# Retention and two feed-forward layers: GpSimd releases the products on zeros and decays one chunk of v, and a low half of x waits for chunk 3's output

## The chip, the core and the metric

The kernel runs on one core of a Trainium2 chip. The metric is the device time of one execution in microseconds (us), taken as the median of several runs. The core has TensorE (PE, with its weight loads PEld), VectorE (DVE), ScalarE (ACT), GpSimd (POOL) and SyncE (SP), which here only issues transfers. Each engine works through its own queue in order and waits on semaphores.

## What is computed

A retention layer (attention without a softmax, with a decay per head) is followed by two feed-forward layers, over 4608 tokens.

```python
rel = pos[:, None] - pos[None, :]
Dmat = np.where(rel >= 0, gamma[:, None, None] ** rel[None, :, :], 0.0)
ret = (scale * np.matmul(q, k.transpose(0, 1, 3, 2))) * Dmat[None]   # batch 8, heads 8, seq 576, dim 64
x = np.matmul(ret, v)  ->  [4608, 512]
h = x @ w_in;  x = (h - np.tanh(h)) @ w_out                           # layer 1, 512 -> 2048 -> 512
h = x @ w_in2; out = (h * (1 / (1 + np.exp(-1.702 * h)))) @ w_out2    # layer 2
```

## The kernel before

The sequence of each batch is cut into five chunks: four of 128 positions and one of 64. `chunks` lists them over all batches, so chunk 4 (counted from 0) is the last, short one of batch 0 and chunk 5 is the first of batch 1. For one chunk four functions run.

- `att_load` loads kT, qT, v and k into buffers of three each.
- `att_decay` multiplies v by a factor per position and head (`dg`). For the chunks 0, 1, 2, 5, 6 and 7 it is one multiplication on DVE (L295), for the others one ACT instruction per head (L300): eight for a chunk of 128, four for a chunk of 64.
- `att_scores` forms the products of k and q (`pj`, L316) and multiplies them by the mask on DVE (`pm`, L321). A "pin", a copy of one element into the bank ahead of the products (L311), ties the start of some chunks to another result: chunk 4 to the state S that chunk 3 leaves, chunk 5 to the first result `w` of the first feed-forward step.
- `att_values` adds the part that comes from the state S of the chunks before and the part within the chunk (`op`, L334), forms the next state (`up` on PE, L348, then two instructions on DVE, L352 and L353), and writes the output: the first 512 columns straight into `x_first` (`xf`, L362), later ones into `xe` (L367), which goes to memory (L371) and comes back as `yf` when its tile of 512 tokens is due (L388).

Four chunks (`LEAD`) run ahead of the feed-forward work. Between them PE is given products on a tile of zeros (`warm`), whose results nobody reads: `fill(src, n)` first writes a zero into one element of `warm`, as an ACT instruction that reads `src` (L719), and then issues n products of 512 columns (L722), which therefore can't run before `src` is there. After chunk 1 there are 5 of them, after chunk 3 there are 12, and `src` is the state S that the chunk just done leaves.

The feed-forward weights come as 64-bit floats in units. `unit_join` turns a unit into 32-bit floats (L176 and L180 on ACT, L178, L181 and L182 on DVE), `unit_split1` splits it into two 16-bit halves: the high half on ACT and the low half on DVE, both in `two` (L186 and L187). Names: `wih` and `wil` are the halves of the first matrix, `woh` and `wol` of the second. x is split in the same way into `xh` and `xl` by `whole(0)` (columns 0 to 383) and `whole(1)` (columns 384 to 511, which hold chunk 3's output).

The feed-forward steps then follow: `mm_in` forms `h` for a pair of blocks of 128 hidden units (24 products of 512 columns: high by high, high by low, low by high, L469), `act1` turns it into `gh` and `gl` on ACT and DVE (L482 to L487, L186, L187), and `mm_out` (L631) forms the output two steps later. The first pair needs the unit called (i, 0) here, that is the first one of the first matrix, the second pair the unit (i, 1). Beside the first tile's eight steps the remaining units are converted and the further chunks of the attention go on, chunk by chunk in one bank of PSUM (`late`). Tile 1 (tokens 512 to 1023) needs the output of the chunks 4 to 8.

The order of the instructions on each engine is not the program's order. It is set when the kernel is built, by a list scheduler that takes what its own estimate of the times calls ready, in the order of the program.

Of the kernel before, what the change touches and what calls it, by code (L numbers as in the profile page):

```python
# [17 lines left out]
AF = mybir.ActivationFunctionType  # L18
ALU = mybir.AluOpType
# [5 lines left out]
B, H, S, D = 8, 8, 576, 64  # L25
NT, DM, DFF = 4608, 512, 2048
P = 128
TT = 512
# [3 lines left out]
NPAIR = H // 2  # L32
# [23 lines left out]
LEAD = 4  # L56
# [39 lines left out]
def small_h(ctx: ExitStack, tc: tile.TileContext, w1i, w1o, w2i, w2o, qt, kt, k, v, dq_d,  # L96
            dv_d, mask_d, dg_d, out, flag):
    nc = tc.nc
    V, A, G, PE, SP = nc.vector, nc.scalar, nc.gpsimd, nc.tensor, nc.sync
# [25 lines left out]
    def pow2(mx, n, least, s, inv):  # L125

        p = scp.tile([P, n], F32, tag=f"p2_{n}", name="p2", bufs=3)
        V.tensor_scalar(out=p, in0=mx, scalar1=least, scalar2=None, op0=ALU.max)
        pi = p.bitcast(I32)
        V.tensor_scalar(out=pi, in0=pi, scalar1=EXPO, scalar2=None, op0=ALU.bitwise_and)  # L130
        V.tensor_scalar(out=s.bitcast(I32), in0=pi, scalar1=-1.0, scalar2=float((254 + 14) << 23),
                        op0=ALU.mult, op1=ALU.add)
        V.tensor_scalar(out=inv.bitcast(I32), in0=pi, scalar1=float(-(14 << 23)), scalar2=None, op0=ALU.add)

    def all_max(src, n, name):
        r = scp.tile([P, n], F32, tag=f"ar{n}", name=name, bufs=4)
        G.partition_all_reduce(r, src, P, RED.max)
        return r

    def most(dst, src, axis=AX.X):  # L140

        V.tensor_copy(out=dst, in_=newest[0])
        V.tensor_reduce(out=dst, in_=src, axis=axis, op=ALU.max, apply_absolute_value=True)
# [119 lines left out]
    att = {}  # L263
# [26 lines left out]
    def att_decay(b, n):  # L290
        s0, T = CHUNKS[n]
        a = att[b, n]
        if b * len(CHUNKS) + n in (0, 1, 2, 5, 6, 7):
            x, w = (0, H) if T == P else (H, NPAIR)
            V.tensor_tensor(out=a.v[:, :w], in0=a.v[:, :w], op=ALU.mult,  # L295
                            in1=dg[:, x : x + w].rearrange("p (a b) -> p a b", b=1).to_broadcast([P, w, D]))
            return
        for h in range(H if T == P else NPAIR):
            x = h if T == P else H + h
            A.activation(out=a.v[:, h], in_=a.v[:, h], func=AF.Copy, scale=dg[:, x : x + 1])  # L300
# [76 lines left out]
    def prep_steps(l, t):  # L377

        j = jobs[l, t] = Obj()

        def load():
            if (l, t) == (1, 0):
                j.src = x_first[0]
            else:
                j.src = yp.tile([P, KD, TT], F32, tag="yf", name=f"yf{l}_{t}")
                for x in range(2) if l == 1 else (slice(None),):
                    x = cut(x) if l == 1 else x
                    SP.dma_start(j.src[:, :, x], (x_d if l == 1 else y_d)[t][:, :, x])  # L388
            if l == 2:
                j.mx = scp.tile([P, 2], F32, tag="mx2", name="mxx", bufs=2)  # L390

        def cut(i):
            return (slice(0, 384), slice(384, TT))[i]

        def reduce(i):
            most(j.mx[:, i : i + 1] if l == 2 else xmost[:, 2 * t + i :][:, :1],
                 j.src[:, 2 * i : 2 * i + 2, :].rearrange("p a b -> p (a b)"))
            if i == 1 and l == 2:
                m1 = scp.tile([P, 1], F32, tag="mx1", name="m1", bufs=4)
                V.tensor_reduce(out=m1, in_=j.mx, axis=AX.X, op=ALU.max)  # L400
                j.r = all_max(m1, 1, "arx")

        def whole(i):
            if i == 0:
                j.xh = xp.tile([P, KD, TT], F16, tag="xh", name=f"xh{l}_{t}")
                j.xl = xp.tile([P, KD, TT], F16, tag="xl", name=f"xl{l}_{t}")
            both(*(x[:, :, cut(i)] for x in (j.xh, j.xl, j.src)))

        def scale_x():
            j.sx = scp.tile([P, 2], F32, tag="sx", name="sx")  # L410
            r4 = scp.tile([P, 1], F32, tag="mx1", name="r4", bufs=4)
            V.tensor_scalar(out=r4, in0=j.r, scalar1=4.0, scalar2=None, op0=ALU.mult)
            pow2(r4, 1, 2.0**-90, j.sx[:, 0:1], j.sx[:, 1:2])

        def both(hi_, lo_, src):
            two(hi_, lo_, src, SX if l == 1 else j.tied)

        def plain():
            j.tied = scp.tile([P, 1], F32, tag="tied", name="tied")
            for x in (newest[0], j.sx[:, 0:1]):  # L420
                V.tensor_copy(out=j.tied, in_=x)
            (p0, t0), (p1, t1), (p2, t2), (p3, t3) = tile_slots(t)
            j.bh = p0.tile([P, 3, 2, 256], F16, tag=t0, name=f"bh{t}")
            j.bl = p1.tile([P, 3, 2, 256], F16, tag=t1, name=f"bl{t}")
            j.th = p2.tile([P, 4, 2, 256], F16, tag=t2, name=f"th{t}")
            j.tl = p3.tile([P, 4, 2, 256], F16, tag=t3, name=f"tl{t}")
            both(j.bh[:, 0], j.bl[:, 0], j.src[:, 0:2, 0:256])
            for x in range(2):
                both(j.bh[:, 1 + x], j.bl[:, 1 + x], j.src[:, 2:4, 256 * x : 256 * x + 256])

        def summed():
            (b11, b12), (b21, b22) = [[j.src[:, 2 * k : 2 * k + 2, 256 * x : 256 * x + 256] for x in range(2)] for k in range(2)]
            V.tensor_tensor(out=b11, in0=b12, in1=b11, op=ALU.subtract)
            V.tensor_tensor(out=b12, in0=b22, in1=b12, op=ALU.subtract)
            V.tensor_tensor(out=b22, in0=b22, in1=b11, op=ALU.subtract)
            V.tensor_tensor(out=b21, in0=b21, in1=b22, op=ALU.subtract)

        def split_sums(i):
            for n, (k, x) in ((0, (0, 0)), (2, (0, 1))) if i == 0 else ((1, (1, 1)), (3, (1, 0))):
                both(j.th[:, n], j.tl[:, n], j.src[:, 2 * k : 2 * k + 2, 256 * x : 256 * x + 256])  # L440

        def scale_g():
            bd = scp.tile([P, 1], F32, tag="bd", name="bd")
            V.tensor_scalar(out=bd, in0=j.r, scalar1=8.0 * DM, scalar2=None, op0=ALU.mult)
            j.sg = scp.tile([P, 2], F32, tag="sg", name="sg")
            pow2(bd, 1, 2.0**-96, j.sg[:, 0:1], j.sg[:, 1:2])
            j.isig = scp.tile([P, 1], F32, tag="isig", name="isig")
            V.tensor_scalar(out=j.isig, in0=j.sx[:, 1:2], scalar1=1 / SW, scalar2=None, op0=ALU.mult)
            j.iy = scp.tile([P, 1], F32, tag="iy", name="iy")
            V.tensor_scalar(out=j.iy, in0=j.sg[:, 1:2], scalar1=1 / SW, scalar2=None, op0=ALU.mult)  # L450

        if l == 1:
            return [load, lambda: whole(0), lambda: whole(1), lambda: reduce(0), lambda: reduce(1)]
        return ([load, lambda: [reduce(i) for i in range(2)], lambda: [scale_x(), scale_g()]],
                [plain, summed, lambda: split_sums(0), lambda: split_sums(1)])
# [207 lines left out]
    chunks = [(b, n) for b in range(B) for n in range(len(CHUNKS))]  # L663
# [7 lines left out]
    dg = ac.tile([P, H + 2 * NPAIR], F32, name="dg")  # L671
# [20 lines left out]
    def next_load(to=None, after=None):  # L692
        if loads1:
            unit_load(1, *loads1.popleft(), to or fp, after)
# [8 lines left out]
    warm = cp.tile([P, TT], F16, name="warm")  # L703
# [12 lines left out]
        att_load(*chunks[i])  # L716
    pre = deque(prep_steps(1, 0))
    def fill(src, n):
        A.activation(out=warm[:1, :1], in_=src, func=AF.Copy, scale=0.0)  # L719
        bank = ps_y.tile([P, TT], F32, tag="y", name="idle")  # L720
        for _ in range(n):
            PE.matmul(bank, warm[:, :P], warm, start=True, stop=True)  # L722

    for i in range(-2, LEAD):
        if i + 2 < LEAD:
            att_decay(*chunks[i + 2])
        if 0 <= i + 1 < LEAD:
            att_scores(*chunks[i + 1], early)
        if i >= 0:
            att_values(*chunks[i], early)  # L730
            if i < 2:
                att_load(*beyond[i + NIP])
                for x in range(2):
                    next_load(tp if i and x else fp, x_first[0][:1, x, P * i :][:, :1])
            if i in (1, LEAD - 1):
                fill(att[0, "S"][:1, 0, :1], 5 if i == 1 else 12)
        if i == 2:
            after = [att[0, LEAD - 1].p[-1][:1, 0, :1]]
    after.append(x_first[0][:1, 0, TT - 1 :])
# [25 lines left out]
    for i in range(n1 + LAG):  # L765
        if i < n1:
            t, p = steps[i]
# [7 lines left out]
            if bg:  # L775
                n = min(6 if t == 0 else 5, len(bg))
# [46 lines left out]
        if i >= LAG:  # L823
            t, p = steps[i - LAG]
# [4 lines left out]
    for n in range(LAG, NTILE * KF // 2):  # L829
        t, p = divmod(n, KF // 2)  # L830
# [827 lines left out]
```

## Time and profile before

| what | value |
|---|---|
| median of 3 runs | 1551.64 us (1550.86 to 1552.01) |
| profiled execution | 1551.14 us, span of its instructions 1549.2 us |
| PE | busy 1533.3 us, 99% of the span |
| DVE | busy 1080.3 us, 70% |
| ACT | busy 827.3 us, 53% |
| POOL | busy 5.6 us, 20 instructions |
| TensorE clock | granted share 0.997 over the span |

The page gives busy times over the span. [...] All times inside the span are counted from its start.

### The profile page before, as it was taken

The numbers are of one execution on the slowest core, as the hardware profiler recorded it, in microseconds if no ns is written. First come the engines' busy times: TensorE is split into PE (matmuls) and PEld (weight loads), VectorE is DVE, ScalarE is ACT, GpSimd is POOL, SyncE is SP. The second block draws the span as 40 slices with busy tenths as digits, with TensorE's granted clock in tenths as the row PEclk, the third lists the DMA queues.
The fourth block names the chain that finished last, engine by engine and source line by source line (L and its number), as shares of the span: only waits on it lengthen the run. The fifth ranks groups of instructions, "written<-read, shape, count | busy, mean of one in ns | idle before, by whom it ended". The sixth has DMA issues, their size and how long they took to land.

```text
span 1549.2 us, 29561 instructions
## 1 busy us (share of the span) xinstructions
PE 1533.3 (99%) x12347; PEld 1024.7 (66%) x12347; DVE 1080.3 (70%) x1718; ACT 827.3 (53%) x1453; POOL 5.6 (0%) x20
## 2 busy tenths in 40 slices
PE   8999999999999999999999999999999999999998
PEld 4554555555455544444444588888888888888887
DVE  7984435544543438888776499797888888887865
ACT  4994545454545446668675455354544454454432
POOL 0000000000000000000000000000000000000000
PEclk9999999999999999999999999999999999999999
DMA  9753324333433234454428243443434433443410
GB/s 358 248 184 110 115 78 139 95 90 96 123 98 90 64 92 167 142 180 163 147 96 319 79 146 115 153 131 119 147 120 128 141 128 120 135 130 106 133 62 30
DMA packets 115278, 205.83 MB, mean 133 GB/s; under 512 B 24768, under 2 KB 56128, under 8 KB 113984
## 3 DMA queue, kind: packets, MB, share of 16 engines
q1 hardware_dynamic: 114848, 203.72, 39.9%
q8 instruction: 99, 1.62, 0.5%
q14 instruction: 43, 0.35, 0.1%
q10 hardware_dynamic: 288, 0.14, 0.0%
HBM read 161.88 MB, written 41.94 MB: 132 GB/s over the span
## 4 chain that ended last, share of the span: by engine, by line
PE 95%; ACT 2%; DMA 1%; DVE 1%; issue 0%; SPq 0%; DVEq 0%; ACTq 0%
PE y L631 23%; PE h L469 23%; PE pr L525 21%; PE yp L560 20%; PE op L334 3%; PE pj L316 2%; PE yk L560 1%; PE op L348 1%; DMA v<-n_v 1%; ACT w L176 1%; PE idle L722 0%; DMA qT<-t_q 0%; ACT w L180 0%; ACT u L486 0%; ACT v L300 0%
## 5 line engine op out<-in xcount | busy, mean ns | idle before, releaser
L525 PEld LDWEIGHTS <-ws 128*128 128x128 f16 x3024 | 295.9, 98 | 36.5 <-issue 1.7
L469 PE MATMUL h<-xh,wih 128*128 128x512 f16 x576 | 218.5, 379 | 0.0
L631 PE MATMUL y<-gl,woh 128*128 128x512 f16 x576 | 218.5, 379 | 0.0
L631 PE MATMUL y<-gh,wol 128*128 128x512 f16 x576 | 218.4, 379 | 0.0
L469 PE MATMUL h<-xl,wih 128*128 128x512 f16 x576 | 218.4, 379 | 0.0
L469 PE MATMUL h<-xh,wil 128*128 128x512 f16 x576 | 218.3, 379 | 0.0
L631 PE MATMUL y<-gh,woh 128*128 128x512 f16 x576 | 217.8, 379 | 0.0
L525 PE MATMUL pr<-th,ws 128*128 128x256 f16 x1152 | 217.4, 273 | 0.3 <-DVE u L539 0.2
L469 PEld LDWEIGHTS <-wih 128*128 128x128 f16 x1152 | 111.4, 98 | 132.0
L631 PEld LDWEIGHTS <-woh 128*128 128x128 f16 x1152 | 111.5, 98 | 131.7
L487 DVE TENSOR_TENSOR wt<-u,wt 128x1024 f32<-128x1024 f32 x72 | 88.1, 1223 | 156.2 <-ACT u L486 156.1
L560 PE MATMUL yp<-wo,gh 128*128 128x256 f16 x1152 | 186.8, 273 | 0.0
L525 PE MATMUL pr<-bh,ws 128*128 128x256 f16 x864 | 170.4, 273 | 0.0
L482 ACT ACTIVATE u<-h 128x512 f32<-128x512 f32 x144 | 85.3, 592 | 152.9 <-PE h L469 152.8
L541 ACT ACTIVATE gs<-u,isig 128x1024 f32<-128x1024 f32 x72 | 82.5, 1146 | 142.5 <-DVE u L540 142.5
L525 PE MATMUL pr<-tl,ws 128*128 128x256 f16 x576 | 157.0, 273 | 0.0
L560 PE MATMUL yp<-wo,gl 128*128 128x256 f16 x576 | 135.4, 273 | 0.0
L186 ACT ACTIVATE gh<-gs,sg 128x1024 f16<-128x1024 f32 x72 | 82.7, 1149 | 91.4 <-DVE gs L544 91.3
L560 PE MATMUL yp<-wo,ringwoh 128*128 128x256 f16 x768 | 126.2, 273 | 0.0
L560 PEld LDWEIGHTS <-gh 128*128 128x128 f16 x1152 | 112.7, 98 | 13.0
L186 ACT ACTIVATE gh<-wt 128x1024 f16<-128x1024 f32 x72 | 76.0, 1056 | 79.1 <-DVE wt L487 79.0
L525 PE MATMUL pr<-bl,ws 128*128 128x256 f16 x432 | 117.4, 273 | 0.0
(141 smaller groups left out, 2324.6 us busy)
## 6 DMA issues: line engine op xcount, KB each, us to landing
ws<-pd SPq DMA_DIRECT2D x144, 448.0 KB, 4.0
f<-in_moe_w_in SPq DMA_DIRECT2D x16, 1024.0 KB, 6.3
f<-in_moe_w_out SPq DMA_DIRECT2D x16, 1024.0 KB, 5.1
yd<-ev SPq DMA_DIRECT2D x36, 256.0 KB, 2.4
yf<-yd SPq DMA_DIRECT2D x9, 1024.0 KB, 5.6
out<-ev SPq DMA_DIRECT2D x36, 256.0 KB, 2.5
kT<-t_k SPq DMA_DIRECT2D x32, 256.0 KB, 3.0
qT<-t_q SPq DMA_DIRECT2D x32, 256.0 KB, 2.9
```

The costliest lines, as they stand in the source:

```text
L176: A.activation(out=half[:, :, 1].bitcast(F16), in_=part[:, :, 3].bitcast(BF16), func=AF.Copy)
L186: A.activation(out=hi, in_=src, func=AF.Copy, scale=scale)
L316: PE.matmul(o, a.kT[hs, hp, :T], a.qT[hs, hp, :T], start=True, stop=True)
L334: PE.matmul(op[64 * c : 64 * c + 64, j, q, c0:c1], w(hp, j), x(hp, j), start=start and not q, stop=stop and q == 1)
L348: PE.matmul(up[half(j), hp, :D], a.k[:, NPAIR * j + hp, :], a.v[:, NPAIR * j + hp, :], start=True, stop=True)
L469: PE.matmul(h, w, x[:, kd, :], start=n == 0, stop=n == 3 * KD - 1)
L482: A.activation(out=u[:, x], in_=h, func=AF.Tanh, scale=isig * NARROW)
L487: V.tensor_tensor(out=w, in0=u, in1=th, op=ALU.mult)
L525: PE.matmul(ps, w, x[:, xi, k, :], start=i == 0, stop=i == 5)
L541: A.activation(out=gs.rearrange("p (a b) n -> p a b n", b=2)[:, 0:4:3], in_=h.rearrange("p (a b) n -> p a b n", b=2), func=AF.Gelu_apprx_s ...
L560: PE.matmul(bank[:, m], ops[a][:, x, m * P : m * P + P], L[2].out[w][:, p, wi, :], start=start and m == 0 and r == 0, stop=stop and m == 1 ...
L631: PE.matmul(ys[m], a, b, start=first and i == 0, stop=last and i == 2)
```

## The change

Three edits, all before or at the start of the feed-forward work.

1. `fill` writes its zero on GpSimd instead of ACT. After chunk 1 it still follows the state that this chunk leaves, with 5 products. After chunk 3 it follows the state that chunk 3 reads, which chunk 2 left, and issues 18 products instead of 12.
2. The decay of chunk 4's v is one GpSimd multiplication of 128x256 instead of four ACT instructions.
3. Before `whole(0)` of the first tile splits x, one element of `xl` is written by DVE from the last column of x, which chunk 3's output writes. So the first low half can't start before that output.

```diff
@@ att_decay
+        if (b, n) == chunks[LEAD]:
+            G.tensor_tensor(out=a.v[:, :NPAIR], in0=a.v[:, :NPAIR], op=ALU.mult,
+                            in1=dg[:, H : H + NPAIR].rearrange("p (a b) -> p a b", b=1).to_broadcast([P, NPAIR, D]))
+            return
@@ whole
+                if (l, t) == (1, 0):
+                    V.tensor_copy(out=j.xl[:1, 0, :1], in_=j.src[:1, 0, TT - 1 :])
@@ fill
-        A.activation(out=warm[:1, :1], in_=src, func=AF.Copy, scale=0.0)
+        G.tensor_scalar(out=warm[:1, :1], in0=src, scalar1=0.0, scalar2=None, op0=ALU.mult)
@@ loop over the first chunks
         if i >= 0:
+            state = att.get((0, "S"))
             att_values(*chunks[i], early)
 ...
-            if i in (1, LEAD - 1):
-                fill(att[0, "S"][:1, 0, :1], 5 if i == 1 else 12)
+            if i == 1:
+                fill(att[0, "S"][:1, 0, :1], 5)
+            elif i == LEAD - 1:
+                fill(state[:1, 0, :1], 18)
```

## Rows read from the trace of the kernel before

**Rows 1.** The page's busy times: us, share of the span, instructions.
```profile
PE 1533.3 (99%) x12347; PEld 1024.7 (66%) x12347; DVE 1080.3 (70%) x1718; ACT 827.3 (53%) x1453; POOL 5.6 (0%) x20
```

**Rows 2.** PE's waits over the whole span: us in total, times, longest.
```profile
PE idle L722 <- ACT warm L719: 4.0, 1, 4.0
...
PE op L334 <- DVE pm L321: 1.1, 1, 1.1
```

**Rows 3.** PE's timeline, 20 to 32 us: start, duration, line, work, idle before.
```profile
20.71 0.67 PE L334 MATMUL op<-qT,S 64*64 64x128 f32 x16 [1.01 <-DVE S L353]
21.17 1.10 PE L334 MATMUL op<-pm,v 64*64 64x64 f32 x32
26.24 4.93 PE L722 MATMUL idle<-warm 128*128 128x512 f16 x12 [3.97 <-ACT warm L719]
31.10 0.68 PE L316 MATMUL pj<-qT,kT 64*64 64x64 f32 x16
```

**Rows 4.** Windows: length, busy time by engine, granted clock, DMA share, GB/s.
```profile
20.50:21.00 0.50, 0.29 (x12) 0.32 (x15) 0.36 (x2) 0.50 (x1) 0.00 (x0) 1.00 0.99 369
23.50:24.00 0.50, 0.00 (x0) 0.00 (x0) 0.50 (x2) 0.00 (x0) 0.00 (x0) 0.84 1.06 399
30.60:30.80 0.20, 0.20 (x3) 0.03 (x1) 0.20 (x1) 0.20 (x2) 0.00 (x0) 0.82 1.07 389
...
35.00:40.00 5.00, 5.00 (x52) 2.42 (x50) 4.97 (x7) 5.00 (x9) 0.00 (x0) 1.00 1.04 392
```

**Rows 5.** ACT's timeline, 25 to 68 us.
```profile
25.02 1.06 ACT L300 ACTIVATE v<-v,dg 128x64 f32<-128x64 f32 x4 [2.47 <-DMA v<-n_v]
...
26.61 1.04 ACT L186 ACTIVATE wih<-w 128x1024 f16<-128x1024 f32 x1
...
34.84 0.60 ACT L482 ACTIVATE u<-h 128x512 f32<-128x512 f32 x1 [2.13 <-PE h L469]
...
67.00 0.60 ACT L482 ACTIVATE u<-h 128x512 f32<-128x512 f32 x1 [1.11 <-PE h L469]
```

**Rows 6.** DVE's timeline, 12 to 35 us.
```profile
12.30 0.68 DVE L295 TENSOR_TENSOR v<-v,dg 128x512 f32<-128x512 f32 x1
...
20.14 0.42 DVE L353 TENSOR_TENSOR S<-S,dg 128x256 f32<-128x256 f32 x1
...
21.68 1.76 DVE L187 SCALAR_TENSOR_TENSOR xl<-xf,xh 128x1536 f16<-128x1536 f32 x1
...
24.35 0.67 DVE L362 TENSOR_TENSOR xf<-op,dq 128x512 f32<-128x512 f32 x1
24.95 1.20 DVE L182 SCALAR_TENSOR_TENSOR w<-f,w 128x1024 int32<-128x1024 int32 x1
26.08 0.13 DVE L171 COPY w<-xf 1x1 int32<-1x1 int32 x1
...
27.97 1.22 DVE L187 SCALAR_TENSOR_TENSOR wil<-w,wih 128x1024 f16<-128x1024 f32 x1
...
32.23 0.69 DVE L295 TENSOR_TENSOR v<-v,dg 128x512 f32<-128x512 f32 x1 [1.17 <-DMA v<-n_v]
...
33.77 1.21 DVE L187 SCALAR_TENSOR_TENSOR wil<-w,wih 128x1024 f16<-128x1024 f32 x1
```

**Rows 7.** POOL's timeline, 4 to 16 us.
```profile
4.53 0.51 POOL L714 COPY mask<-mask 64x64 f32<-64x64 f32 x2 [4.10 <-DMA mask<-c_mask]
12.45 0.70 POOL L158 COPY f<-xf 1x1 int32<-1x1 int32 x2 [7.41 <-DVE xf L362]
15.68 0.29 POOL L158 COPY f<-xf 1x1 int32<-1x1 int32 x2 [2.53 <-DVE xf L362]
```

**Rows 8.** Chain that ended last, in order of time: start, us, what.
```profile
31.89 5.29 PE h L469 x24
...
37.80 5.29 PE h L469 x24
...
114.50 0.70 DVE xe L367
```

## The prediction, made before the changed kernel was run

> **What bounds the kernel now.** I read the page first: PE is busy 99% of the span [rows 1]. So the end is set by PE's own work plus the time in which PE is idle or does work that nobody reads. PE's waits come next. The longest is 4.0 us before the products on zeros, and the one that stands latest of any size, 1.1 us, is before the `op` of a later chunk [rows 2]. Both lie in the first 123 us; behind that PE follows its own queue.
>
> PE's timeline shows what stands at the first of them [rows 3]. Chunk 3's last products run from 21.17 for 1.10 us, so PE is free at 22.27. It then waits 3.97 us for the zero, because ACT writes it behind the decay of chunk 4, which starts at 25.02 when v has landed [rows 5]. The 12 products then take 4.93 us, 0.41 us each, while a product of the same width costs 5.29 / 24 = 0.22 us in the feed-forward work [rows 8]. [...] Chunk 4's scores follow at 31.10 [rows 3], and the feed-forward work starts at 31.89 [rows 8].
>
> Last I looked for what the first `h` really needs. The low half of unit (i, 0) is the last of its inputs: 27.97 + 1.22 = 29.19 [rows 6]. PE starts 2.7 us after that, only because the products on zeros are in front.
>
> **The products on zeros.** The new `src` is the state that chunk 2 left, written at 20.14 + 0.42 = 20.56 [rows 6]. POOL's price for one element is between 0.29 / 2 = 0.15 us and 0.70 - 0.15 = 0.55 us [rows 7], so the zero is there at 20.7 to 21.2, or within another us if DVE is in its way; PE is occupied to 22.27. I take no wait at all. Then 18 products run from 22.3 at the clock that hasn't fallen yet: 18 x 0.22 = 4.0, to 26.3. Chunk 4's scores and the head of its `op`, 0.79 us up to 31.89 in the profile, follow: PE is free for `h` at 27.1. The 5 products after chunk 1 cost the same as before: POOL's zero comes at about the same time as ACT's, if it is not queued behind the two copies that wait for chunk 1's output at 15.68 [rows 7].
>
> **The first `h`.** The marker in `xl` moves the first low half of x (1.76 us at 21.68) behind chunk 3's output, which ran at 24.35 although its products were done at 22.27; the output can thus start 2.1 us earlier [rows 6]. The work in front of the low half of (i, 0) is the same, plus one copy of 0.13 us, the price of the marker at 26.08. The best order takes out what stands between that marker and the low half, 27.97 - 26.21 = 1.76 us, except for the second low half of x, a third of the first, 0.6 us: ready at 29.19 + 0.13 - 1.16 = 28.2. The worst puts the join of 1.20 us last, so that ACT's high half of 1.04 us [rows 5] has nothing beside it: 29.19 + 0.13 + 1.04 = 30.4. I take the time of before plus the copy, 29.3. The first four products of the pair (two for each bank) need no low half of the weights, 4 x 0.22 = 0.9 us, so PE's work counts from 28.4 (27.3 to 29.5). Against 31.89 that is 3.5 us earlier (2.4 to 4.6).
>
> **ACT and POOL.** ACT loses the four decays (1.06 us) and the zero. It was waiting for v anyway (2.47 us [rows 5]), so the gain is only that the second high half of x no longer stands behind v; it is in the 3.5 us. POOL's multiplication isn't in the trace. Its nearest row is the copy of 64 columns, 0.51 / 2 = 0.25 us, which is the lower bound; four times the columns give 1.0 us as the upper one, and I take that [rows 7]. It starts when v has landed, at 25.0, and ends at 26.0, and its reader, chunk 4's `op`, ran after the first pair of `h` at 37.2 (31.89 + 5.29) [rows 8], so `h` hides it. Without that cover it would cost at most 1.0 us. No transfer moves: SP's queue has the same issues, and chunk 7's v waits for chunk 4's `op`, which comes earlier.
>
> POOL may be held by DVE: a pair of its copies took 0.70 us at 12.45 and 0.29 us at 15.68, and in the first case DVE ran a multiplication of two SBUF operands from 12.30 to 12.98 [rows 6, 7]. [...]
>
> **What becomes of the 3.5 us.** The second pair of `h` starts at 37.80 and needs the low half of (i, 1) for its third product, at 37.80 + 2 x 0.22 = 38.2; that half is ready at 33.77 + 1.21 = 34.98 [rows 6, 8]. DVE stands in front of it until v lands at 32.23, which the change doesn't move. So 3.2 us fit here. From there DVE and ACT are as full as PE: 4.97 and 5.00 of 5.00 us [rows 4]. ACT waited 2.13 us for `h` at 34.84 and 1.11 us at 67.00 [rows 5], so it can follow PE by 2.1 us before its own work is in the way. What PE waits for last is tile 1's input: chunk 8's output at 114.50 [rows 8], two transfers, the split and the mask of chunk 9, before which PE idles 1.1 us [rows 2]. Chunk 5's scores are pinned to the first result of the first pair, so this chain moves with `h` as far as ACT and DVE let it. Its lower bound is what ACT has left late, 1.1 us; its upper bound is the 3.5 us and the 1.1 us that PE then waits no longer, 4.6 us. The nearest rows are ACT's 2.1 us and the 3.2 us of the low half; I take their middle, 2.6 us.
>
> The profiled execution took 1551.14 us: 1551.14 - 2.6 = 1548.5. The median of the runs is 0.5 us above the profiled one, so 1549.0.
>
> **Rivals.** First, tile 1's input doesn't move (0.20). For it: DVE and ACT are full, and ACT has only 1.11 us of wait at 67.00. PE then waits longer before tile 1, and 0 to 1.1 us remain: 1550.5 to 1551.6, taken as 1550.8.
>
> Second, all of it is kept and the last wait closes too (0.19). For it: gl, gh and the masks depend on PE and come earlier with it, and conversions can give way. 1551.6 - 4.6 = 1547.0.
>
> Third, the clock falls again (0.07). Between 27.1 and 28.4 PE has 1.3 us without work. A gap of 1.01 us left the clock at 1.00, one of 1.6 us didn't [rows 3, 4]. [...]
>
> Fourth, POOL's multiplication holds DVE (0.04). It falls on the joins at 25 to 26 us and costs its 1.0 us; with DVE in its late order 2.4 - 1.0 = 1.4 us remain: 1550.2. [...]
>
> Fifth, chunk 8's output comes later than now (0.07). The orders on DVE are made anew, and this output stands among joins of 1.20 us each; three more of them in front make it 3.6 us late. From the moment tile 1's input comes later than in the profile PE's early start is worth nothing, and each us counts: 1555.2, slower. Against it: the scheduler takes this chain first, by the program's order.
>
> Sixth, the change doesn't do what it says and the zero doesn't come early (0.03). If POOL's queue has chunk 4's decay first, the zero comes at 26.0 as now. [...]
>
> **Chances and range.** The forecast has 0.40, with a spread of about a us on either side. A measurement here can tell 0.2%, 3.1 us, from no change; faster than that is below 1548.5. That takes the second rival and somewhat under half of the forecast, 0.17: 0.36. Slower is most of the fifth rival, 0.06. The rest, 0.58, is within 0.2%. The range runs from the second rival with its spread, 1546.0, past the first rival and to 1552.2; what is left out is the fifth, part of the sixth and the tails.
>
> **What would show it.** Right: 18 products from about 22.3 with the clock at 1.00 all through, `h` at 27 to 29.5, PE's wait before tile 1 not above some 2 us. The first step is wrong if PE idles between 22.3 and the products, the second if `h` starts after 29.5, the third if DVE waits beside POOL's multiplication, the last if PE waits before the second or third pair of `h`, or if tile 1 starts at 122 us or later as now. The forecast falls if the orders on DVE and ACT after 35 us are other ones than these.

## The result, and the profile after

The changed kernel takes 1560.73 us (1560.26 to 1564.41, six runs), the kernel before 1551.07 us beside it (six runs): 1.0065 times as long, 95% interval 1.0052 to 1.0078. That is 9.7 us slower, outside the predicted range. The profiled execution took 1560.32 us, with a span of 1558.5 us against 1549.2.

First the list of PE's waits after the change (us in total, times, longest). It answers to [rows 2].

```profile
PE idle L728 <- POOL warm L725: 7.7, 1, 7.7
PE h L475 <- DVE xl L187: 1.9, 1, 1.9
PE op L338 <- DVE S L357: 1.5, 1, 1.5
PE pj L320 <- DMA qT<-t_q: 1.4, 1, 1.4
...
PE op L338 <- DVE pm L325: 1.1, 1, 1.1
```

The wait of 4.0 us on ACT's zero is gone, as it should be. In its place stands one of 7.7 us, on the same kind of product but on POOL's zero, and a new one of 1.9 us at the first `h`. POOL's timeline (start, duration, work, and in brackets how long POOL was idle before it and who ended that) shows where the first one comes from. It answers to [rows 7].

```profile
12.45 0.70 POOL L158 COPY f<-xf 1x1 int32<-1x1 int32 x2 [7.18 <-DVE xf L366]
21.71 0.26 POOL L725 TENSOR_SCALAR warm<-S 1x1 f16<-1x1 f32 x1 [8.57 <-issue]
21.94 0.30 POOL L158 COPY f<-xf 1x1 int32<-1x1 int32 x2
30.54 0.53 POOL L725 TENSOR_SCALAR warm<-S 1x1 f16<-1x1 f32 x1 [8.30 <-DVE S L357]
31.02 0.61 POOL L299 TENSOR_TENSOR v<-v,dg 128x256 f32<-128x256 f32 x1
```

The zero itself costs 0.26 us, within the predicted 0.15 to 0.55. But POOL stands still for 8.57 us ahead of it, and what ended that is "issue": nothing the trace shows. The second zero has 0.53 us and no such gap, since its 8.30 us are a wait for the state. The built order of POOL's instructions has one more line there than the program asks for, just ahead of the first zero (number in the order, line, operation, what it works on; the extra line is an `ISA` one without operands):

```
7 L158 COPY f_279<-xf 1x1
8 L158 COPY f_282<-xf 1x1
9 L725 ISA
10 L725 TENSOR_SCALAR warm<-S 1x1
11 L158 COPY f_351<-xf 1x1
...
13 L725 TENSOR_SCALAR warm<-S 1x1
14 L299 TENSOR_TENSOR v_4_349<-v_4_349,dg 128x256
15 L137 ISA
16 L137 ISA arx<-m_7701 128x1
```

In the built program this line carries the name `PseudoReloadLibraryIndex`, with the index 0 here and 1 ahead of the reductions (L137), and it stands ahead of POOL's wait for the state. So the 8.57 us, which begin where the copies end (12.45 + 0.70 = 13.15), are called the load from here on; what POOL does in them no row shows. In the kernel before the first line of this kind after the start is the one of L137, ahead of a reduction at 824 us, where POOL has been idle for 808 us anyway. So before this change POOL copies and fills, but does no arithmetic, until 824 us.

Here is what the 8.57 us do to PE, which had to issue five products right there. PE's timeline, to be held against [rows 3]:

```profile
22.03 2.32 PE L728 MATMUL idle<-warm 128*128 128x512 f16 x5 [7.70 <-POOL warm L725]
24.28 2.08 PE L320 MATMUL pj<-qT,kT 64*128 64x128 f32 x16
...
30.50 0.67 PE L338 MATMUL op<-qT,S 64*64 64x128 f32 x16 [1.52 <-DVE S L357]
30.96 1.10 PE L338 MATMUL op<-pm,v 64*64 64x64 f32 x32
32.00 4.06 PE L728 MATMUL idle<-warm 128*128 128x512 f16 x18
35.98 0.44 PE L320 MATMUL pj<-qT,kT 64*64 64x64 f32 x6
36.36 0.60 PE L475 MATMUL h<-xh,wih 128*128 128x512 f16 x2
...
39.33 0.38 PE L475 MATMUL h<-xl,wih 128*128 128x512 f16 x1 [1.88 <-DVE xl L187]
```

The scores of chunk 3 stand behind the five products in PE's order, and all of the attention stands behind those scores. Chunk 3's `op` starts at 30.50 instead of 20.71 [rows 3]: 9.8 us lost. The windows (length, busy time by engine with counts, granted clock, DMA share, GB/s; order PE, PEld, DVE, ACT, POOL) show that the clock went with it.

```profile
16.00:17.00 1.00, 0.00 (x0) 0.00 (x0) 0.00 (x0) 0.00 (x0) 0.00 (x0) 0.60 1.06 383
24.00:25.00 1.00, 1.00 (x7) 0.72 (x8) 0.00 (x0) 0.00 (x0) 0.00 (x0) 0.50 0.94 344
32.00:33.00 1.00, 1.00 (x8) 0.50 (x6) 0.71 (x2) 0.35 (x1) 0.00 (x0) 1.00 0.99 318
41.00:42.00 1.00, 1.00 (x4) 0.31 (x3) 1.00 (x2) 0.31 (x1) 0.00 (x0) 0.50 0.00 0
```

PE has nothing to do from 14.3; in 16 to 17 the granted clock is 0.60, and at 24 to 25 it is 0.50: chunk 3's scores take 2.08 us there, instead of the 1.16 us of before at clock 1.00. Then the good part of the change follows: 18 products in 4.06 us at clock 1.00, with no wait before them, where the kernel before spent 3.97 us of waiting and 4.93 us on 12. That wins back 5.3 us: the first `h` comes at 36.36 against 31.89 [rows 8], 4.5 us late. Then the first pair of `h` loses 4.2 us again. It waits 1.88 us for the low half of x, and behind that the clock is at 0.50 once more (41 to 42). The second pair starts at 46.48 against 37.80 [rows 8], 8.7 us late. The span grew by 9.3.

One table holds what the experiments below are about (us in the profiled execution, and in the last two rows the medians of the timed runs). The last three columns are the experiments 1, 9 and 12.

| | before | after | load early | load early, no marker | and one join later |
|---|---|---|---|---|---|
| chunk 3's `op` | 20.71 | 30.50 | 21.04 | 20.80 | 20.91 |
| first `h` | 31.89 | 36.36 | 26.89 | 27.28 | 27.32 |
| second pair | 37.80 | 46.48 | 38.09 | 37.38 | 34.20 |
| chunk 5's scores | 43.01 | 51.77 | 43.57 | 44.37 | 45.88 |
| median | 1551.07 | 1560.73 | 1552.98 | 1550.84 | 1553.45 |
| median of before beside it | | 1551.07 | 1551.67 | 1551.32 | 1551.44 |

Chunk 5's scores run in two halves, of which the table gives the first, except in experiment 9, where they run in one piece: there they end at 45.5, before the change at 45.8.

### The profile page after: what moved, and what is told of

Read it like the earlier page. It is cut to its first block, busy times and chain, and to the rows that moved or that the text cites. A ratio compares the mean times of both kernels' runs of the same rounds, so it can differ in the third digit from the quotient of the medians.

```text
span 1558.5 us, 29575 instructions
## 1 busy us (share of the span) xinstructions
PE 1535.8 (99%) x12353; PEld 1025.2 (66%) x12353; DVE 1081.3 (69%) x1719; ACT 825.0 (53%) x1447; POOL 7.0 (0%) x23
## 3 DMA queue, kind: packets, MB, share of 16 engines
q8 instruction: 99, 1.62, 0.4%
## 4 chain that ended last, share of the span: by engine, by line
PE 93%; DVE 2%; ACT 2%; DMA 1%; issue 1%; SPq 0%; POOL 0%; ACTq 0%; DVEq 0%
PE y L637 23%; PE h L475 22%; PE pr L531 21%; PE yp L566 20%; PE op L338 3%; PE pj L320 2%; PE yk L566 1%; PE op L352 1%; DMA qT<-t_q 1%; DVE w L182 1%; ACT v L304 0%; ACT w L176 0%; DMA v<-n_v 0%; DVE wt L493 0%; DVE f L181 0%
```

## The experiments

**1. One instruction more, at the start.** A single multiplication on an element of its own, as POOL's first work; everything else as in the changed kernel.

```diff
     V.memset(warm, 0.0)
+    early_op = cp.tile([P, 1], F32, name="early_op")
+    G.memset(early_op, 0.0)
+    G.tensor_scalar(out=early_op[:1, :1], in0=early_op[:1, :1], scalar1=0.0, scalar2=None, op0=ALU.mult)
```

> The changed kernel, with one more GpSimd multiplication of one element right at the start, on a tile that nobody else reads, so that whatever GpSimd needs ahead of its first multiplication is done before the first zero is asked for. If the 8.6 us ahead of the first zero are a one-time preparation of GpSimd (theory), they move to about 0.5 to 9 us, the zero for the 5 products comes at about 14.0 instead of 21.7, PE no longer waits 7.7 us, and the run is 8 to 12 us faster than the changed kernel: 1548 to 1552 us. If GpSimd is slow with any multiplication there, or held by DVE or by the transfers that are under way (rival), the wait stays at 13 to 22 us and the run at about 1560.

Measured: 1552.98 us against 1551.67, ratio 1.0010 (1.0001 to 1.0019), 1 us above the 1548 to 1552 that I expected. POOL's timeline:

```profile
9.25 0.26 POOL L713 TENSOR_SCALAR early_op<-early_op 1x1 f32<-1x1 f32 x1 [8.43 <-issue]
...
14.25 0.20 POOL L728 TENSOR_SCALAR warm<-S 1x1 f16<-1x1 f32 x1 [0.82 <-DVE S L357]
...
25.27 0.61 POOL L299 TENSOR_TENSOR v<-v,dg 128x256 f32<-128x256 f32 x1 [3.68 <-DMA v<-n_v]
```

The stillness moved to the new instruction, 8.43 us from 0.8 on, where nobody waits for POOL; the zero comes at 14.25 and POOL has no gap of that kind any more. So it belongs to POOL's first multiplication and not to this zero. It accounts for 9.66 - 1.31 = 8.4 of the 9.7 us.

The 1.3 us that remain are slower than before, not the 2.6 us of gain that I forecast. That needed a second search.

**2. The same zero by a copy.** POOL copies the state's element instead of multiplying it by zero, and chunk 4's decay goes back to ACT, so that POOL does no arithmetic early. The element of `warm` then holds a value of the state and not zero; nobody reads these products.

```diff
-        if (b, n) == chunks[LEAD]:
+        if False:
...
-        G.tensor_scalar(out=warm[:1, :1], in0=src, scalar1=0.0, scalar2=None, op0=ALU.mult)
+        G.tensor_copy(out=warm[:1, :1], in_=src)
```

> The changed kernel with the element of the tile of zeros written by a GpSimd copy of the state's element instead of a multiplication by zero (it is then not zero, but nobody reads the products), and with chunk 4's decay on ACT again. GpSimd then has no multiplication before the last stage. Theory: copies ran on it without a gap at 12.45 and 15.68, so no preparation, the 5 products start at 14.3, the 18 at 22.3, and the run takes 1547 to 1551 us. If GpSimd as such is late with this element (rival), PE waits some us before the 5 products as in the changed kernel.

Measured: 1552.83 us against 1551.67, ratio 1.0010 (1.0001 to 1.0019). The copies took 0.18 and 0.55 us at 13.94 and 20.85, with no stillness ahead. The mechanism is the expected one, the time is 1.8 us above the 1547 to 1551 of the theory: the kernel ends where the first experiment does, by another way around the load.

**3. The load alone, with PE not behind it.** In the kernel before, one multiplication on POOL behind chunk 1's state.

```diff
+                if i == 1:
+                    G.tensor_scalar(out=alone[:1, :1], in0=att[0, "S"][:1, 0, :1], scalar1=0.0, scalar2=None, op0=ALU.mult)
```

> The kernel before, with one GpSimd multiplication of one element added after chunk 1's state, whose result nobody reads. It measures the preparation by itself, away from PE's queue: theory, about 8.6 us on GpSimd from 13.2, with the two copies ahead of the next weight loads behind it, at 22 instead of 15.7, so that the loads of two units start about 4.5 us later. PE's products on zeros stay where they were. If the weights have that much to spare, 1551 to 1552 us; if not, up to 1556. If the wait ahead of the zero came from PE or ACT (the zero also waits on them), there is no such gap here.

Measured: 1552.10 us, ratio 1.0005 (0.9996 to 1.0014). The load is there:

```profile
21.90 0.26 POOL L739 TENSOR_SCALAR alone<-S 1x1 f32<-1x1 f32 x1 [9.09 <-DVE w L178]
22.12 0.31 POOL L158 COPY f<-xf 1x1 int32<-1x1 int32 x2
```

It holds up the two copies behind it, which release two loads of weights (22.12 instead of 15.68 [rows 7]), and costs nothing that can be told, as expected. So what costs in the changed kernel is that PE stands behind POOL, not the late weights.

**4. The zero on ACT, the decay on POOL.**

```diff
-        G.tensor_scalar(out=warm[:1, :1], in0=src, scalar1=0.0, scalar2=None, op0=ALU.mult)
+        A.activation(out=warm[:1, :1], in_=src, func=AF.Copy, scale=0.0)
```

> The changed kernel with the zeros written by ACT as before; the earlier state, the 18 products, the decay of chunk 4 on GpSimd and the marker stay. Theory: the one-time preparation now stands ahead of GpSimd's decay, from about 16 to 24.6 us, beside v's transfer, and nobody waits for it, so 1547 to 1551 us. If the marker or the order that it makes on DVE is what costs the 9 us (rival), this run is slow too, about 1558 to 1561.

Measured: 1552.93 us, ratio 1.0011 (1.0002 to 1.0020). POOL's multiplication (25.11, 0.62 us) is now its first arithmetic. The built order has the extra line ahead of it, so its load falls into the 9.19 us in which POOL stands idle before v; the trace can't part the two. DVE's low half of x, which started at 25.29 beside it, took 2.05 us; in the kernel before it took 1.76 [rows 6]. So it was 0.3 us longer beside POOL's multiplication. The rival (the marker costs the 9 us) is out; the theory's 1547 to 1551 was missed by 1.9 us.

**5. Without the marker.** The copy kernel of experiment 2, less the edit that makes the low half of x wait for chunk 3's output.

```diff
-                if (l, t) == (1, 0):
-                    V.tensor_copy(out=j.xl[:1, 0, :1], in_=j.src[:1, 0, TT - 1 :])
```

> The run with the copied element (zeros by a GpSimd copy, chunk 4's decay on ACT, 18 products behind chunk 2's state) without the marker in xl. On DVE the join of unit (i, 1) (1.2 us) then stands ahead of the multiplication of chunk 5's v again, as in the kernel before, and not behind its wait for the transfer. Theory: the marker's order is what ate the gain, the low half of (i, 1) is ready at about 35 instead of 38, the second pair of h starts at 34 to 36 instead of 37.8, and the run takes 1548 to 1550.5 us. Rival: ACT, or PE's own gaps (the clock, 1.7 us) ate it; then the run stays at 1552 to 1553.

Measured: 1551.10 us against 1551.49, ratio 0.9999 (0.9990 to 1.0008); with the marker it was 1.0010. What is left of the change is neither faster nor slower than before, where I expected 1548 to 1550.5. The profiled execution took 1552.43 us: in it an early transfer of q holds PE up, and chunk 3's `op` is at 22.90, so its times lie some 2 us later than in the others. PE's timeline shows what the second pair waits for:

```profile
38.72 0.38 PE L473 MATMUL h<-xh,wih 128*128 128x512 f16 x1 [2.66 <-ACT wt L487]
```

And ACT's timeline shows why that is late:

```profile
36.39 1.36 ACT L176 ACTIVATE w<-f 128x1024 f16<-128x1024 bf16 x1 [2.18 <-DVE wil L187]
37.62 0.56 ACT L486 ACTIVATE u<-h 128x512 f32<-128x512 f32 x1
38.09 0.59 ACT L487 ACTIVATE wt<-h 128x512 f32<-128x512 f32 x1
```

PE is done with what stands in front at 36.1 and waits for ACT's `wt` (the second tanh on the first product of the pair). `h` has two banks of PSUM, and the second pair needs the first of them back. ACT stood idle from 34.2 to 36.39: in its order the join of unit (i, 2) is ahead of the tanh, and that waits until DVE's low half of (i, 1) gives back one of the two buffers of joined weights; DVE is late because it stood waiting for chunk 5's v. Experiment 9 shows the same chain without the early delay.

ACT has these instructions in another order here than in the kernel before, where both tanh stand ahead of that join. ACT's timeline before, behind the tanh at 34.84 [rows 5]:

```profile
35.34 0.59 ACT L483 ACTIVATE wt<-h 128x512 f32<-128x512 f32 x1
35.81 1.38 ACT L176 ACTIVATE w<-f 128x1024 f16<-128x1024 bf16 x1
```

So the change gave ACT a new order too: the scheduler put the join ahead of the tanh, and with that the bank behind chunk 5's v.

**6. The marker alone**, in the kernel before.

```diff
+                if (l, t) == (1, 0):
+                    V.tensor_copy(out=j.xl[:1, 0, :1], in_=j.src[:1, 0, TT - 1 :])
```

> The kernel before with the marker alone: zeros by ACT at 26 us, 12 products, chunk 4's decay on ACT. DVE's order puts the join of (i, 1) behind the multiplication of chunk 5's v, as in the changed kernel. Theory: slower than before by what the low half of (i, 1) comes later (about 3 us) less the 3.2 us that it had to spare, and by what follows for ACT: 1552 to 1554 us. Rival (the marker is harmless and only the early products cost): 1551 to 1551.8.

Measured: 1556.15 us (1553.87 to 1558.62), ratio 1.0035 (1.0023 to 1.0047). It costs by itself, and more than the 1552 to 1554 that I expected; the profiled execution is the fastest of the six, so its trace holds 2.4 of the 4.7 us at most. DVE's order shows what changed: the join of unit (i, 1) (L182) is now behind chunk 5's decay, for whose v DVE stands still 2.64 us, where before it was ahead, at 29.83.

```profile
29.04 0.69 DVE L181 TENSOR_SCALAR f<-f 128x1024 int32<-128x1024 int32 x1
32.38 0.69 DVE L295 TENSOR_TENSOR v<-v,dg 128x512 f32<-128x512 f32 x1 [2.64 <-DMA v<-n_v]
32.99 0.69 DVE L181 TENSOR_SCALAR f<-f 128x1024 int32<-128x1024 int32 x1
33.59 1.22 DVE L182 SCALAR_TENSOR_TENSOR w<-f,w 128x1024 int32<-128x1024 int32 x1
```

The low half of (i, 1) falls from 33.77 [rows 6] to 36.79. In the first experiment it is at 36.83, by the same order.

**7. Chunk 5's decay on POOL too**, in the kernel of the first experiment, so that DVE doesn't stand waiting for v.

```diff
-            V.tensor_tensor(out=a.v[:, :w], in0=a.v[:, :w], op=ALU.mult,
+            (G if b * len(CHUNKS) + n == 5 else V).tensor_tensor(out=a.v[:, :w], in0=a.v[:, :w], op=ALU.mult,
```

> The changed kernel with the early GpSimd multiplication (1552.98 us), and chunk 5's decay on GpSimd instead of DVE; the marker stays. DVE then doesn't stand 1.9 us for chunk 5's v with two joins behind it. Theory: the low half of (i, 1) comes 2.5 to 3 us earlier than in that run, the second pair of h starts at about 36 instead of 38.1, 1550 to 1551.5 us. Rival (the gaps of PE and the clock): no change, 1553.

Measured: 1552.57 us, ratio 1.0008 (0.9999 to 1.0017). The second pair started at 36.74, 1.35 us earlier than in the first experiment. The second half of that pair then waited 2.47 us, up to 41.96, for ACT's `wt` on the second half of the first pair, which stands behind two joins there. The wait only moved, and the 1550 to 1551.5 of the theory were missed.

**8. 28 products instead of 18**, in the kernel of experiment 2, so that PE has no gap before the low half of x.

```diff
-                fill(state[:1, 0, :1], 18)
+                fill(state[:1, 0, :1], 28)
```

> The run with the copied element (1552.83 us) with 28 products on zeros instead of 18, so that PE is busy until the second low half of x is there and the clock doesn't fall in front of the first pair of h. The 10 products more cost 2.2 us, of which some 1.8 us were idle; the slow products at 0.43 us, some 8 of them, are saved, 1.7 us. Theory (the second pair is held by DVE and ACT): the first pair is done 1 to 1.5 us earlier, the second still starts at about 37.8, and the time is the same, 1552 to 1553.3. Rival (the fallen clock is what ate the gain): 1550.5 to 1551.5.

Measured: 1555.16 us, ratio 1.0025 (1.0015 to 1.0036). The first pair's products stood 0.22 us apart; it was done at about 34.4 and gave nothing: the second started at 39.92, after 4.73 us of waiting for ACT's `wt`. In ACT's built order the join is ahead of the tanh here too, other than in experiment 2. So the wait is the one that the theory named, but the second pair didn't stay at 37.8 nor the time within 1552 to 1553.3, and with another order on ACT this run doesn't tell what the fallen clock alone costs.

**9. All of the change but the marker, load early.** The first experiment's kernel without the two lines of experiment 6.

> All of the change but the marker, and GpSimd's first multiplication made early on an element of its own (as in the first experiment). Theory (the marker's order is what made the first experiment slower than before; the load is hidden): the 18 products run from 22.3 at full clock, GpSimd's decay of chunk 4 at about 25.1 takes 0.6 us, the join of (i,1) is again ahead of chunk 5's decay, the first h at 29 to 30, and the second pair waits for the tanh of the first until about 37.8: 1551.0 (1550.3 to 1551.8), no difference from before. Rival (it was the preload or GpSimd's decay that cost the 1.2 us, not the marker): 1552.5 to 1553.2, as with the marker.

Measured: 1550.84 us against 1551.32, ratio 0.9999 (0.9990 to 1.0008): the theory held. Between this and the first experiment only the marker differs: 1.31 + 0.48 = 1.8 us, and the times of the two (1550.32 to 1551.53 and 1552.48 to 1553.45) don't meet. The first `h` is at 27.28, 4.6 us earlier than before, and the chain of experiment 5 takes it back: ACT stands idle in front of its join.

```profile
35.05 1.36 ACT L176 ACTIVATE w<-f 128x1024 f16<-128x1024 bf16 x1 [2.63 <-DVE wil L187]
```

PE's timeline at the second pair:

```profile
37.38 0.59 PE L473 MATMUL h<-xh,wih 128*128 128x512 f16 x1 [3.10 <-ACT wt L487]
37.76 0.63 PE L473 MATMUL h<-xl,wih 128*128 128x512 f16 x1
```

The windows around it:

```profile
36.00:37.00 1.00, 0.00 (x0) 0.00 (x0) 1.00 (x3) 1.00 (x3) 0.00 (x0) 0.85 1.04 391
37.00:40.00 3.00, 2.62 (x7) 0.96 (x7) 2.96 (x4) 3.00 (x7) 0.00 (x0) 0.50 1.04 395
```

PE idles 3.10 us before the second pair, the clock falls in 36 to 37, and the pair's first seven products stand 0.41 us apart instead of 0.22, another 1.3 us. In these windows DVE and ACT are busy all the time. The third pair starts at 46.08 against 45.95 before, with the same products in front of it, so nothing is left of the 4.6 us there. POOL's decay of chunk 4 took 2.44 us here, from 25.40, and DVE's low half of (i, 0), which met its end, 1.62 instead of 1.22.

**10. And chunk 5's decay on POOL as well.** Experiment 9 with the line of experiment 7.

> As the run before, and chunk 5's decay goes to GpSimd too, so that DVE's joins no longer stand behind the transfer of chunk 5's v. Theory (the second pair waits for a tanh that stands in order on ACT behind a join, and that for DVE's low half of (i,1), and that for chunk 5's v): without that wait the low half of (i,1) is done 1.2 to 1.4 us earlier, at about 34.0, ACT's join starts there, the tanh is done at about 36.5, and the second pair starts at 36 to 37 instead of 37.8 to 38.7: 1549.5 to 1550.5 if later pairs keep it. Rival (ACT and DVE are full behind it, as the third group was when the marker was in): the gain stands as a longer wait before a later group of h, and 1551 to 1552.5 remains.

Measured: 1550.98 us, ratio 1.0000 (0.9991 to 1.0009). The rival held, and at a new price. DVE no longer stands at chunk 5's v, but its low half of (i, 1) meets POOL's multiplication. POOL's timeline:

```profile
32.83 1.33 POOL L295 TENSOR_TENSOR v<-v,dg 128x512 f32<-128x512 f32 x1 [5.76 <-DMA v<-n_v]
```

DVE beside it:

```profile
33.17 2.07 DVE L187 SCALAR_TENSOR_TENSOR wil<-w,wih 128x1024 f16<-128x1024 f32 x1
```

It took 2.07 us instead of 1.21 [rows 6], so it was done at 35.2, as before (34.98), and the second pair began at 37.61.

**11. Another bank for the second pair.** Experiment 5 with the first half of the second pair in a bank of `y`, which is free then.

```diff
...
-            act1(t, 2 * p, [mm_in(1, t, 2 * p + x, ps_h) for x in range(2)])
+            act1(t, 2 * p, [mm_in(1, t, 2 * p + x, *((ps_y, "y") if i == 1 and not x else (ps_h,))) for x in range(2)])
```

> The fifth experiment's kernel (no marker, zero by a copy), with the first product of the second pair in a bank of PSUM from the pool of y, which nobody uses then, so it does not wait for the first pair's tanh. Theory (the bank is the last wait there): the first two products of the second pair run before 37, no wait above 1 us on ACT before them, and the second pair's later products, at about 37.5 instead of 38.7, wait for the weights' low half or the other bank; 1549.5 to 1550.6 if ACT can follow. Rival (ACT and DVE are full: taking the bank's wait away only moves it to a later pair): the wait on ACT before h in 40 to 60 us grows by the same us and the time stays at 1551.0 to 1552.

Measured: 1552.64 us, ratio 1.0009 (0.9999 to 1.0018). This settles nothing: the scheduler put the half in the old bank first, which still waited 2.55 us for the tanh, at 36.84.

**12. The join behind the first tanh.** Experiment 9, in which the join of unit (i, 2) waits for the first pair's first tanh. So the tanh doesn't stand behind it.

```diff
...
+        first.append(th[:1, 0, :1].bitcast(F32))
...
+            if i == 0:
+                work[2] = lambda: next_join(first[0])
```

> As the ninth experiment (all of the change but the marker, load early), and the join of unit (i,2) waits for the first tanh of the first pair, so that on ACT this tanh no longer stands behind a join that waits for DVE's low half of (i,1). Theory (it was this order on ACT that held the first pair's bank of PSUM, and with it the second pair): the tanh starts when the first pair's products end, at about 33.7, the bank is free at about 34.8, the second pair starts at 34.5 to 36 instead of 37.4, the clock does not fall, and 1 to 2 us of the early start are kept: 1549.0 to 1550.2. Rival (DVE's and ACT's work after the first pair is itself the bound, in whatever order): the wait comes back before the third pair's or a later pair's h, or before tile 1, as 2 to 3 us on ACT or DVE, and the time stays at 1550.5 to 1552.

Measured: 1553.45 us, ratio 1.0018 (1.0009 to 1.0027). The first half of the theory held and the second half fell, and the time lies above the rival's 1550.5 to 1552 too. ACT's first tanh is done at 33.38, and the second pair starts without any wait, 3.6 us earlier than before. PE's timeline from there:

```profile
34.20 0.39 PE L473 MATMUL h<-xh,wih 128*128 128x512 f16 x1
...
39.52 0.46 PE L338 MATMUL op<-pm,v 64*64 64x64 f32 x16 [1.83 <-DVE pm L325]
40.42 0.38 PE L473 MATMUL h<-xh,wih 128*128 128x512 f16 x1 [0.43 <-ACT wt L487]
```

The window behind it:

```profile
41.00:42.00 1.00, 1.00 (x4) 0.42 (x3) 0.77 (x2) 1.00 (x2) 0.00 (x0) 0.50 1.02 395
```

It waits for chunk 4's mask, made by DVE behind conversions of the weights, the clock falls, and chunk 5's scores are 2.9 us later than before. So ACT's order, and with it the bank, was the gate of the second pair. That DVE's and ACT's own work is the next gate isn't shown, since the edit has a price of its own: the join now starts behind a copy of one element that DVE reaches only at 36.96, behind chunk 6's decay. ACT's timeline after the first tanh:

```profile
36.53 1.06 ACT L186 ACTIVATE woh<-w 128x1024 f16<-128x1024 f32 x1 [3.15 <-DVE w L182]
...
38.11 1.33 ACT L176 ACTIVATE w<-f 128x1024 f16<-128x1024 bf16 x1
```

So ACT stood idle for 3.15 us, and its part of the join of (i, 2) came 3.1 us later than in experiment 9.

## Why the prediction failed, point by point

**The five products after chunk 1: the step that failed first.** I wrote that they "cost the same as before" and took POOL's price from its copies. The zero itself did cost 0.20 to 0.61 us; what I lacked was that POOL had done no arithmetic before, so no row of before could hold the price of its first one. I bounded an operation by rows of another kind and never asked for an upper end that contains something new. 8.4 of the 9.7 us are this. My sixth rival had POOL's queue ahead of a zero, but of the later one, with the decay in it. From the forecast (2.6 us faster) to the result (9.7 us slower) it is 12.3 us: 8.4 for the load, 1.8 for the marker, and 2.1 of gain that isn't kept even without both (experiment 9).

**The 18 products.** Right. They were taken at 0.22 us each, from 22.3 on, at a clock that hadn't fallen yet. In the kernel before it fell and rose again within two of the windows of [rows 4]; these stand ahead of them and behind them:

```profile
23.00:23.50 0.50, 0.00 (x0) 0.00 (x0) 0.50 (x2) 0.00 (x0) 0.00 (x0) 1.00 1.10 395
...
24.00:24.50 0.50, 0.00 (x0) 0.00 (x0) 0.50 (x3) 0.00 (x0) 0.00 (x0) 0.50 1.01 387
...
30.40:30.60 0.20, 0.20 (x2) 0.12 (x1) 0.20 (x1) 0.20 (x2) 0.00 (x0) 0.50 1.00 369
...
30.80:31.00 0.20, 0.20 (x2) 0.00 (x0) 0.20 (x1) 0.20 (x1) 0.00 (x0) 1.00 1.36 461
```

My estimate from these shares is a fall from 1.00 to 0.50 near 23.8, 1.6 us after PE's last product, and a rise near 30.7, 4.4 us after the 12 products began. With the load out of the way the 18 products run from 22.3 to 22.5 in 4.06 us at clock 1.00 (experiments 1 and 9), and even in the changed kernel they take 4.06 us, only 9.7 us later than forecast.

**The first `h`.** The size was right without the marker: in experiment 9 the first product that needs `wil` runs at 28.97 with three before it, which counts from 28.97 - 0.66 = 28.3; I had 28.4. That agreement is luck in part: I had taken DVE's times of before, and they stayed only without the marker. With it, in experiment 1, the first product that waits runs at 29.93 with two before it, so from 29.5, the late end of my range. The reason was wrong. I let the marker make room for chunk 3's output, 2.1 us of it. DVE put a join there instead (L182), and the output started at 24.78 in experiment 1, later than before (24.35 [rows 6]) and than without the marker (24.28). With the marker the low half of x delays the first pair by 1.9 us, and DVE's new order puts the join of (i, 1) behind a transfer. In these builds the scheduler filled the gap that the marker opened with what else was ready; my worst case had that join last, and it came first, ahead of the output; I looked no further down the queue.

**POOL's multiplication.** Taken at 0.25 to 1.0 us; it took 0.61 us in the changed kernel and in experiment 1, but 2.44 and 1.51 us from start to end in the experiments 9 and 10, where a join of DVE's (L182) was under way when it began. It was hidden, as said. The fourth rival's direction, for which no row of before stood, did show: DVE's instructions beside POOL's multiplication took 0.3, 0.4 and 0.9 us longer (experiments 4, 9 and 10). That it costs DVE its whole length, 1.0 us, was my estimate, and no run shows that; no gain or loss of the total hung on it.

**"So 3.2 us fit here": the step that failed second.** I took the low half of (i, 1) for the last input of the second pair. It is the bank of PSUM, which ACT's tanh gives back; in the new order the tanh stands on ACT behind a join, and through it behind the same low half and chunk 5's v (experiments 5, 9 and 11). With that chain the second pair starts at about 37 (37.38 in experiment 9), which is where it started before. I had seen ACT's wait of 2.13 us before the tanh [rows 5] and called it room; it was room only in the order of before, in which the tanh has no join in front. My last sign, "The forecast falls if the orders on DVE and ACT after 35 us are other ones than these", is what happened, and I had given it no chance of its own.

**"Between 1.1 and 4.6 us are kept."** None is. Experiments 9 and 12 give the first `h` 4.6 us and experiment 12 the second pair 3.6 us, and neither is faster than before at the end. The window of 35 to 40 us [rows 4], with DVE at 4.97 and ACT at 5.00 of 5.00 us, suggests that their work is the limit in whatever order; that isn't shown, since ACT stood idle for 2.63 us ahead of the join in experiment 9 and for 3.15 us in experiment 12.

**The rivals.** Tile 1's input was never the gate: the gain was lost by the third pair, some 70 us ahead of it, and in experiment 9 PE waited 0.73 us before the scores at 104.65, and not again up to 130 us. The fall of the clock did happen, in the changed kernel and in experiment 1 after 1.9 us without work: some eight products 0.43 us apart instead of 0.22, 1.7 us. Chunk 8's output did not decide.

**What stays open.** Whether an order of DVE's and ACT's work exists that keeps the 4.6 us wasn't found; the four that were tried (experiments 7, 10, 11 and 12) don't, of which 11 didn't do what it was meant to and 12 paid for its own copy. An order with ACT's tanh ahead of the join and chunk 4's mask at its place of before (DVE had it at 33.44 then, and at 40.30 in experiment 9), without such a copy, wasn't tried. No version beat the kernel before by more than can be told. That the extra line in POOL's order is the load itself rests on its name and on where it stands: it is there whenever the stillness is, and in experiment 2 neither is there before the reductions.

## What to carry to other kernels

Before moving work to an engine, ask whether that engine has done this kind of operation before in the program; if not, its first one can cost microseconds (8 to 9 us on POOL in these runs), so do one on a spare element where nobody waits, or use a kind that it has done already. When you free an engine, follow the next consumer to everything that it waits for, the buffers and banks that others must give back among them, and through the order of the engine that gives them back; that order may be a new one in the changed build. And a constraint given to a scheduler changes the whole order behind it, so look for what has slid behind a transfer.

## What the runs showed of the hardware

- GpSimd stood still for 7.97 to 9.09 us ahead of its first arithmetic (8.57 after the change; 8.43, 9.09, 8.54, 8.27, 8.38 and 7.97 in the experiments 1, 3, 7, 9, 10 and 12), also from 0.8 us on, where hardly anything else had begun. Copies, conversions by copy and fills had no such time (in experiment 2 a pair of copies took 0.29 us and the conversions 0.18 and 0.55, released by DVE; in experiment 1 a fill took 0.10). A multiplication of two tensors right behind one by a constant needed none either (0.61 us at 31.02 after the change).
- POOL's multiplication of chunk 4's v took 0.61 us after the change and in the experiments 1 and 7, and 0.62 in experiment 4; with a join of DVE's (two operands from SBUF) under way at its start it took 2.44 (experiment 9) and 1.51 (experiment 10), and in experiment 12 it took 1.55. DVE's low halves beside a multiplication on POOL took 2.05 us instead of 1.76 (experiment 4), 1.62 instead of 1.22 (experiment 9) and 2.07 instead of 1.21 (experiment 10).
- In these runs the length of a gap without work on PE didn't decide by itself whether the clock fell: 2.66 us in experiment 5 left it at 1.00 (36 to 43), and behind 1.88 us in experiment 7 the products stood 0.22 us apart, while 2.55 us in experiment 11 and 1.94 us in experiment 1 were followed by 0.50 (37.3 to 40.5 and 31 to 33.5).
